# Gate and value products of the second feed-forward layer as seven products of 2x2 blocks

## The chip, the core and the metric

The kernel runs on one core of one Trainium2 chip. The metric is the device time of one execution in microseconds (us); lower is better. The core's engines work side by side and are tied by semaphores: TensorE (PE, its weight loads PEld), VectorE (DVE), ScalarE (ACT), GpSimd (POOL), and SyncE (SP), which issues the DMAs here.

## What is computed

The reference filters two sequences by an FFT and passes the 6016 tokens of 256 channels through two feed-forward layers. The change is in the last one:

```
x = irfft(rfft(x) * F)                      # 2 x 3008 tokens, 256 channels
x = silu(x @ w_in) @ w_out                  # layer 1: 256 -> 2048 -> 256
g, v = x @ w_gate, x @ w_val                # layer 2: 256 -> 1536, twice
out = (silu(g) * v) @ w_out2                # 1536 -> 256
```

## The kernel before

Weights arrive as float64, are rounded to float32 on the chip and split into a high and a low part of type float32r. The activations are split in the same way. A product of two split operands is three matmuls (high by high, high by low, low by high, the list `PARTS`), which add up in PSUM.

Tokens go in 12 blocks of 512 (the last has 384), `NBLK` and `size(t)`. Layer 2 runs block by block; within a block a unit `(2, t, f)` makes 128 of the 1536 hidden features. `m2_in` (L492 to L503) makes a unit's gate in one PSUM bank and its value in another: two halves of the 256 channels by three matmuls is 6 matmuls of 512 columns for each, 12 in all (L427). ACT takes silu of the gate (L499), DVE multiplies by the value (L501), and `split` makes the high part on ACT (L434) and the low part on DVE (L435). `m2_out` multiplies by `w_out2`: for each 128 tokens one matmul of 512 columns (L512) and one of 256 (L516), into four banks that the block keeps until its last unit. Their sums leave by ACT (L525), DVE (L526) and a DMA.

The order is written out in the main loop: unit i's `m2_in`, then the `m2_out` of unit i - 4 (`LAG`). A table `todo` puts other steps ahead of a unit: loading and converting weights (`load_w`, `conv_a`, `conv_b`, `conv_c`), and, for each block of layer 2, `load_x2` and `split_x2` (L488 on ACT, L489 on DVE), ten and five units ahead. Each engine keeps the order in which its instructions were written, so an instruction that waits holds up all that stands behind it on its engine. SP's DMAs form one such order too. Tiles named "mid" come from one pool of 35 buffers; PSUM has four buffers for intermediate results (`psum`) and four for sums (`acc_p`).

All weights of layer 2 are made from float64 while layer 1 runs and stay in SBUF until the end.

Of the kernel before, what the change touches and what calls it, by code (L numbers as in the profile page):

```python
# [92 lines left out]
def fft_filter_mlp_kernel(  # L93
# [39 lines left out]
    csp = cp.tile([P, 2, 352], F32R, name="csp")  # L133
# [16 lines left out]
    # the tensor engine runs at half its clock until it has been busy for a while  # L150
# [8 lines left out]
    t2t = [cp.tile([P, 4, P], F32, name=f"t2t{i}") for i in range(2)]  # L159
# [172 lines left out]
    def s4(c, halves=(0, 1), bank=psum):  # L332
        """Four columns, which one or two blocks of tokens take."""
# [47 lines left out]
    def conv_a(key, q, half, on_act=True):  # L381
# [4 lines left out]
        m = stp.tile([P, 512], U32, tag="m", name="m", bufs=4)  # L386
# [22 lines left out]
    def conv_c(key, q, half):  # L409
# [67 lines left out]
    x2_of = {}  # L477
# [5 lines left out]

    def split_x2(t):
        n = size(t)
        x = mid([P, 2, 512], "xh", F32R), mid([P, 2, 512], "xl", F32R)
        s = x2_of.pop(t)
        nc.scalar.copy(x[0][:, :, :n], s[:, :, :n])  # L488
        nc.vector.tensor_tensor(x[1][:, :, :n], s[:, :, :n], x[0][:, :, :n], op=ALU.subtract)  # L489
        xt_of[t] = x  # L490

    def m2_in(t, f):  # L492
        n = size(t)
        gps = psum("g")
        mm_in(gps, "g", f, xt_of[t], n)
        vps = psum("v")
        mm_in(vps, "v", f, xt_of[t], n)
        u = tp.tile([P, 512], F32, tag="u", name="sg")
        nc.scalar.activation(u[:, :n], gps[:, :n], AF.Silu)  # L499
        u2 = tp.tile([P, 512], F32, tag="u", name="gv")  # L500
        nc.vector.tensor_tensor(u2[:, :n], vps[:, :n], u[:, :n], op=ALU.mult)  # L501
        hid[2, t, f] = split(u2, n)

    def m2_out(t, f):
        nt = size(t) // P
        if f == 0:
# [32 lines left out]
    units += [(2, t, f) for t in range(NBLK) for f in range(12)]  # L539
# [8 lines left out]
    def weights(i, key, q, step=1):  # L548
        """Loads and converts one pair of halves in stages."""
# [23 lines left out]
    for t in range(NBLK):  # L573
        i = begin[2, t]
        at(i - 10, load_x2, t)
        at(i - 5, split_x2, t)
    i = 80
    for key, q in (("g", 0), ("v", 0), ("o2", 0), ("g", 1), ("v", 1), ("o2", 1)):
        weights(i, key, q, 4)
        i += 8  # L580
    for i, key in ((14, "g"), (10, "v"), (6, "o2")):
        weights(END1 - i, key, 2, 2)

    # the second batch's transform, between the units of the first batch's blocks
# [9 lines left out]
    for h in range(12):  # L594
# [15 lines left out]
    LAG = 4  # L610
    with tc.manual_schedule():
# [118 lines left out]
        late["p"] = pool("late", 6)  # L730
# [74 lines left out]
```

## Time and profile before

| what | value |
|---|---|
| timed runs | 1240.48, 1243.15, 1245.9 us; median 1243.15 |
| profiled execution, span from first to last instruction | 1240.2 us |
| PE busy | 1214.2 us, 98% of the span |
| PEld, DVE, ACT, POOL busy | 1008.4, 598.7, 556.8, 170.2 us |
| granted TensorE clock, mean | 0.993 of full speed (2.4 GHz) |
| first gate matmul of layer 2, last DMA issue | 645.3 us, 1236 us after the span's start |

The profile is of one execution, for which a span is given and no device time apart from it; the median of the timed runs lies 2.95 us above that span, for what lies around it. Matmuls are pipelined and their ends are modelled, so the distance from one matmul's start to the next tells what one costs, not its duration.

### The profile page before, as it was taken

Reading aid. Unit: us, or ns where it says so; the run is one execution under the profiler, and the core shown is the slowest. Engines: PE = TensorE matmul, PEld = TensorE weight load, DVE = VectorE, ACT = ScalarE, POOL = GpSimd, SP = SyncE. Lnnn points to the kernel's source line nnn. Section 1 sums busy time; section 2 is a strip of 40 time slices with the busy share of each in tenths; the row PEclk is TensorE's granted clock in tenths of the full one; section 3 lists DMA queues with packets and bytes.
Section 4 is the critical chain, followed back from the end, with each engine's and each line's share of the span. In section 5 each row is a group of like instructions: output and inputs, shape, how many; then the busy total and the mean of one; then the engine's idle time right before and its main releaser. Section 6 shows DMA issues by size and latency. Waiting matters only on the chain.

```text
span 1240.2 us, 14660 instructions
## 1 busy us (share of the span) xinstructions
PE 1214.2 (98%) x5772; PEld 1008.4 (81%) x5772; DVE 598.7 (48%) x890; ACT 556.8 (45%) x985; POOL 170.2 (14%) x120
## 2 busy tenths in 40 slices
PE   7999899999999999999999999999999999999998
PEld 6567678888888888888888888888888888888898
DVE  4889957674354552222384333343343433433433
ACT  3565666665455555444454333233333333333332
POOL 3545633240012210000040000000000000000000
PEclk9999999999999999999999999999999999999999
DMA  9861532332023120010130010000010100000000
GB/s 235 241 194 49 124 110 70 122 89 77 17 69 94 34 77 18 1 43 18 35 119 30 1 34 18 18 35 17 17 35 1 35 17 17 35 17 13 18 1 30
DMA packets 44740, 69.00 MB, mean 56 GB/s; under 512 B 2848, under 2 KB 27936, under 8 KB 44672
## 3 DMA queue, kind: packets, MB, share of 16 engines
q1 hardware_dynamic: 44672, 68.08, 18.5%
q8 instruction: 45, 0.74, 0.3%
q14 instruction: 23, 0.19, 0.0%
HBM read 46.31 MB, written 21.76 MB: 55 GB/s over the span
## 4 chain that ended last, share of the span: by engine, by line
PE 86%; DVE 3%; POOL 3%; issue 2%; ACT 1%; DMA 1%; POOLq 0%; DVEq 0%
PE h L427 17%; PE acc L466 17%; PE g L427 16%; PE v L427 15%; PE acc L512 11%; PE acc L516 5%; PE s L337 2%; PE s L173 2%; POOL m L407 1%; POOL w L417 1%; DMA x<-in_xp_dram 1%; PE s L170 1%; DVE h L435 1%; POOL fl L195 1%; ACT w L416 1%
## 5 line engine op out<-in xcount | busy, mean ns | idle before, releaser
L466 PE MATMUL acc<-h,w 128*128 128x512 f32 (+1 forms) x1152 | 291.2, 388 | 2.7 <-DVE h L435 2.7
L427 PE MATMUL h<-xh,w 128*128 128x512 f32 (+1 forms) x768 | 268.2, 390 | 2.9 <-ACT w L416 1.6
L435 DVE TENSOR_TENSOR h<-u,h 128x512 fp32r<-128x512 f32 (+1 forms) x192 | 149.5, 780 | 219.0 <-ACT h L434 218.6
L466 PEld LDWEIGHTS acc<-h,w 128*128 128x128 f32 x1152 | 216.9, 189 | 45.6 <-DVE h L435 3.1
L501 DVE TENSOR_TENSOR gv<-v,sg 128x512 f32<-128x512 f32 (+1 forms) x144 | 98.0, 680 | 256.2 <-PE v L427 253.8
L512 PE MATMUL acc<-w,h 128*128 128x512 f32 x564 | 204.0, 396 | 0.0
L427 PE MATMUL g<-xh,w 128*128 128x512 f32 (+1 forms) x576 | 200.1, 388 | 2.5 <-ACT u L454 2.5
L427 PE MATMUL v<-xh,w 128*128 128x512 f32 (+1 forms) x576 | 198.1, 384 | 0.0
L434 ACT CAST h<-gv 128x512 fp32r<-128x512 f32 (+1 forms) x144 | 88.1, 612 | 210.0 <-DVE gv L501 210.0
L454 ACT ACTIVATE u<-h 128x512 f32<-128x512 f32 (+1 forms) x192 | 112.5, 586 | 144.7 <-PE h L427 144.5
L427 PEld LDWEIGHTS h<-xh,w 128*128 128x128 f32 x768 | 144.5, 188 | 33.1 <-ACT w L416 2.0
L499 ACT ACTIVATE sg<-g 128x512 f32<-128x512 f32 (+1 forms) x144 | 84.7, 589 | 174.5 <-PE g L427 174.5
L516 PE MATMUL acc<-w,h 128*128 128x256 f32 x564 | 157.9, 280 | 0.0
L427 PE MATMUL h<-xl,w 128*128 128x512 f32 (+1 forms) x384 | 148.4, 386 | 0.0
L435 DVE TENSOR_TENSOR h<-gv,h 128x512 fp32r<-128x512 f32 (+1 forms) x144 | 98.1, 681 | 97.6 <-ACT h L434 97.6
L427 PEld LDWEIGHTS g<-xh,w 128*128 128x128 f32 x576 | 108.0, 188 | 27.3 <-ACT u L454 3.1
L427 PEld LDWEIGHTS v<-xh,w 128*128 128x128 f32 x576 | 107.9, 188 | 21.2
L512 PEld LDWEIGHTS acc<-w,h 128*128 128x128 f32 x564 | 105.9, 188 | 23.7
L434 ACT CAST h<-u 128x512 fp32r<-128x512 f32 (+1 forms) x192 | 117.5, 612 | 6.1
L427 PE MATMUL g<-xl,w 128*128 128x512 f32 (+1 forms) x288 | 112.3, 390 | 0.0
L427 PE MATMUL v<-xl,w 128*128 128x512 f32 (+1 forms) x288 | 110.7, 384 | 0.0
L516 PEld LDWEIGHTS acc<-w,h 128*128 128x128 f32 x564 | 106.4, 189 | 5.0
(69 smaller groups left out, 1002.9 us busy)
## 6 DMA issues: line engine op xcount, KB each, us to landing
raw<-in_w_out_dram SPq DMA_DIRECT2D x14, 512.0 KB, 6.1
zt<-d SPq DMA_DIRECT2D x16, 384.0 KB, 5.0
x<-in_xp_dram SPq DMA_DIRECT2D x15, 384.0 KB, 9.1
d<-z SPq DMA_DIRECT2D x11, 512.0 KB, 3.3
d<-x SPq DMA_DIRECT2D x22, 256.0 KB, 2.1
x<-d SPq DMA_DIRECT2D x11, 512.0 KB, 3.2
out_dram<-ob SPq DMA_DIRECT2D x11, 512.0 KB, 2.9
raw<-in_w_in_dram SPq DMA_DIRECT2D x8, 512.0 KB, 9.6
```

The lines of the kernel that those rows point to most:

```text
L170: nc.tensor.matmul(o, cst[:k, c0:c1], x, start=True, stop=True)
L173: nc.tensor.matmul(o, csp[:k, mp_, c0:c1], x[xp_], start=(i == 0), stop=(i == 2))
L337: nc.tensor.matmul(ps[:, g, 94 * i:94 * (i + 1)], zt_of[c // 4, g][:, 2 * (c % 4) + i, :], c4, start=True, stop=True,)
L427: nc.tensor.matmul(ps[:, :n], wt[key, f // 4, g][:, wpart, o:o + P], x[xpart][:, g, :n], start=(g == 0 and k == 0), stop=(g == 1 and k == 2),)
L434: nc.scalar.copy(h[:, 0, :n], u[:, :n])
L435: nc.vector.tensor_tensor(h[:, 1, :n], u[:, :n], h[:, 0, :n], op=ALU.subtract)
L454: nc.scalar.activation(u[:, :n], ps[:, :n], AF.Silu)
L466: nc.tensor.matmul(acc[1, t][m][:, :n], w[:, wpart, o:o + 128], h[:, xpart, :n], start=(f == 0 and k == 0), stop=(f == 15 and k == 2),)
L499: nc.scalar.activation(u[:, :n], gps[:, :n], AF.Silu)
L501: nc.vector.tensor_tensor(u2[:, :n], vps[:, :n], u[:, :n], op=ALU.mult)
L512: nc.tensor.matmul(a.rearrange("p (l d) -> p l d", l=2), h[:, 0, i * P:(i + 1) * P], w[:, :, f % 2, :], start=(f == 0), stop=False, skip_g ...
L516: nc.tensor.matmul(a[:, D:], h[:, 1, i * P:(i + 1) * P], w[:, 0, f % 2, :], start=False, stop=(f == 11), skip_group_check=True,)
```

## The change

Layer 2's gate and value now use a Strassen form (with the sums shared as in Winograd's variant). Two hidden-feature groups of 128 that lie 256 apart (f and f + 2) and the two halves of a block's tokens form a 2x2 product: weights of 2 channel halves by 2 feature groups, times activations of 2 channel halves by 2 token halves. The plain way takes eight block products, this one seven. A block product is three matmuls of 256 columns instead of being a half of three matmuls of 512.

A unit `m2_unit(t, q, j, outs)` makes both feature groups, so a block has 6 units instead of 12. Per unit PE does 42 matmuls of 256 columns (7 products, 3 parts, gate and value) where two old units had 24 of 512, and the same two `m2_out`. The seven products land in three of the four PSUM buffers (`xs[0]`, `xs[1]`, `y`). What Strassen adds between them is done by ACT (two copies `s` out of PSUM), DVE (`u2`, two additions in place in PSUM, `u3`, the first half of `c`) and POOL (the second half of `c`). The second feature group's silu, product, cast and low part (on POOL) are kept in `rest` and run inside the next unit.

The sums of activations are made by POOL for each block (`prep_x2`, four subtractions of 256 columns, ahead of unit 4 of the block before) and split ahead of unit 5 (`split_x2`, now on 1792 columns instead of 1024). The sums of weights are made during layer 1 on POOL and ACT (`comb_a`, `comb_b`, `comb_c`), written to DRAM (27 DMAs of 512 KB, those of `w_out2` among them), and read back from 18 units before the end of layer 1 on (27 DMAs, `load_2`). The conversions start at the same unit as before (80), and end at unit 173 of the 192 of layer 1. Up to that start all engines' instructions stand as they did. Pools that only the transform and the conversions need are closed earlier to make room.

```diff
     def conv_c(key, q, half):
...
+        if key == "o2":
+            nc.sync.dma_start(do2[q][half], w.rearrange("p l f -> p (l f)").bitcast(F32))
...
+    def comb_a(key, q):
+        v = pair[key, q].bitcast(F32)
+        s = sums[key, q] = mid([P, 4, 256], "ws")
+        sub = lambda o, a, b: nc.gpsimd.tensor_tensor(o, a, b, op=ALU.subtract)
+        nc.gpsimd.tensor_tensor(s[:, 0], v[:, 0, 256:], v[:, 1, 256:], op=ALU.add)
+        sub(s[:, 1], s[:, 0], v[:, 0, :256])
+        sub(s[:, 2], v[:, 0, :256], v[:, 0, 256:])
+        sub(s[:, 3], v[:, 1, :256], s[:, 1])
...
     def split_x2(t):
...
+        for hi, lo, v in (
+            (u[:, 0, :, :n], u[:, 1, :, :n], x[:, :, :n]),
+            (u2[:, 0, :n], u2[:, 1, :n], x[:, 1, n:2 * n]),
+            (h[:, :, :n], l[:, :, :n], r[:, :, :n]),
+        ):
+            nc.scalar.copy(hi, v)
+            nc.vector.tensor_tensor(lo, v, hi, op=ALU.subtract)
...
+    def m2_unit(t, q, j, outs):
...
+        if old:
+            old[0]()
+        for i in range(2):
+            product(xs[i][:, cols[0]], KV[i], q, j, 1, t, first=True)
+            product(xs[i][:, cols[1]], KV[i], q, j, 5, t)
+            nc.scalar.copy(s[:, i, :, :n], xs[i].rearrange("p (l k) -> p l k", l=2)[:, :, :n])
+            if old:
+                old[1 + i]()
...
+        for i in range(2):
+            product(yv[:, i], KV[i], q, j, 6, t, first=(i == 0))
+        nc.vector.tensor_tensor(u2, yv, s[:, :, 0, :n], op=ALU.add)
+        if old:
+            old[3]()
+        outs(0)
+        for i in range(2):
+            product(xs[i][:, cols[0]], KV[i], q, j, 2, t)
+            product(xs[i][:, cols[1]], KV[i], q, j, 3, t, last=True)
+            o = xs[i][:, cols[1]]
+            nc.vector.tensor_tensor(o, o, u2[:, i], op=ALU.add)
...
+        nc.scalar.activation(half(g1), half(xs[0]), AF.Silu)
+        for i in range(2):
+            product(yv[:, i], KV[i], q, j, 7, t)
+        nc.vector.tensor_tensor(u3, yv, s[:, :, 0, :n], op=ALU.add)
+        nc.gpsimd.tensor_tensor(c[:, :, 1, :n], u3, s[:, :, 1, :n], op=ALU.add)
+        nc.vector.tensor_tensor(half(g1), half(xs[1]), half(g1), op=ALU.mult)
+        outs(1)
...
+        nc.scalar.copy(pack(h[:, 0]), half(g1))
+        for i in range(2):
+            product(yv[:, i], KV[i], q, j, 4, t, last=(i == 1))
...
+        def c21():
+            nc.vector.tensor_tensor(c[:, :, 0, :n], yv, s[:, :, 0, :n], op=ALU.add)
+            nc.vector.tensor_tensor(pack(h[:, 1]), half(g1), pack(h[:, 0]), op=ALU.subtract)
...
+        rest.append((c21, silu, cast, low))
...
+    for t in range(1, NBLK):
+        later(t - 1, 3, load_x2, t)
+        later(t - 1, 4, prep_x2, t)
+        later(t - 1, 5, split_x2, t)
```

Line numbers in the rows that follow are those of each kernel's own file. On PE, in the middle of layer 2, one unit of the kernel before is this (L427 the gate `g` and value `v`, L512 and L516 the `m2_out` of an earlier unit):

```order
L427 MATMUL g<-xh,w 128x512
L427 MATMUL g<-xl,w 128x512
L427 MATMUL g<-xh,w 128x512 x2
L427 MATMUL g<-xl,w 128x512
L427 MATMUL g<-xh,w 128x512
L427 MATMUL v<-xh,w 128x512
L427 MATMUL v<-xl,w 128x512
L427 MATMUL v<-xh,w 128x512 x2
L427 MATMUL v<-xl,w 128x512
L427 MATMUL v<-xh,w 128x512
L512 MATMUL acc_6525<-w,h 128x512
```

And the middle of a unit of the changed kernel on PE, from the last matmul of `outs(0)` over the products 2 and 3 to the first of product 7 (`xg`, `xv` are `xs[0]`, `xs[1]`):

```order
L693 MATMUL acc_6755<-w_5632,h 128x256
L602 MATMUL xg<-xu,w_5067 128x256 x3
L602 MATMUL xg<-xu_6987,w_5087 128x256 x2
L602 MATMUL xg<-xu_6987,w_5107 128x256
L602 MATMUL xv<-xu,w_5127 128x256 x3
L602 MATMUL xv<-xu_6987,w_5147 128x256 x2
L602 MATMUL xv<-xu_6987,w_5167 128x256
L602 MATMUL y<-xrh,w_5087 128x256
L602 MATMUL y<-xrl,w_5087 128x256
L602 MATMUL y<-xrh,w_5107 128x256
L602 MATMUL y<-xrh,w_5147 128x256
```

Each product now has its own three matmuls of half the width, and the bank `xg` is written in two visits, with ACT's copy of it between them.

On DVE, at the place where a block's activations are split (L489 before, L589 after), the kernel before has one instruction between two units:

```order
L435 TENSOR_TENSOR h<-gv,h 128x512
L489 TENSOR_TENSOR xl<-x_8274,xh 128x1024
L501 TENSOR_TENSOR gv<-v,sg 128x512
L435 TENSOR_TENSOR h<-gv,h 128x512
```

The changed kernel has three, ahead of the addition L664 (first half of `c`) that the unit before left over:

```order
L650 TENSOR_TENSOR sg<-xv,sg 128x512
L589 TENSOR_TENSOR xu<-x_6807,xu 128x512
L589 TENSOR_TENSOR xu_6987<-x_6807,xu_6987 128x256
L589 TENSOR_TENSOR xrl<-xr,xrh 128x1024
L664 TENSOR_TENSOR c<-y,s 128x2x256
L665 TENSOR_TENSOR h<-sg,h 128x512
L671 TENSOR_TENSOR sg<-c,sg 128x512
L634 TENSOR_TENSOR u_6902<-y,s 128x512
```

On ACT the casts of that split (L588) stand, at the same place, between the last cast of a unit (L658) and the first copy `s` of the next (L627):

```order
L658 CAST h<-sg 128x512
L588 CAST xu<-x_6807 128x512
L588 CAST xu_6987<-x_6807 128x256
L588 CAST xrh<-xr 128x1024
L627 COPY s<-xg 128x512
L668 ACTIVATE sg<-c 128x512
L627 COPY s<-xv 128x512
L672 CAST h<-sg 128x512
```

So a unit's leftover work, and the copies out of PSUM that PE waits for, stand behind the split on both engines.

## Rows read from the trace of the kernel before

**Rows 1.** Windows: stretch, then busy us of PE, PEld, DVE, ACT, POOL (instructions), clock.

```profile
243.00:636.00 393.00, 393.00 (x1843) 331.12 (x1842) 175.13 (x280) 209.17 (x364) 55.09 (x40) 1.00 0.18 55
636.00:690.00 54.00, 51.53 (x253) 44.31 (x252) 28.23 (x40) 23.57 (x42) 7.87 (x6) 1.00 0.08 27
690.00:1192.00 502.00, 502.00 (x2423) 420.72 (x2422) 192.91 (x293) 167.56 (x292) 0.00 (x0) 1.00 0.06 20
800.00:900.00 100.00, 100.00 (x484) 83.80 (x483) 38.31 (x58) 33.31 (x58) 0.00 (x0) 1.00 0.06 22
```

**Rows 2.** Timeline in layer 2, one `m2_out`: start, duration, engine, line.

```profile
901.22 0.39 PE L512 MATMUL acc<-w,h 128*128 128x512 f32 x1
...
901.45 0.28 PE L516 MATMUL acc<-w,h 128*128 128x256 f32 x1
901.45 0.19 PEld L512 LDWEIGHTS acc<-w,h 128*128 128x128 f32 x1
...
901.56 0.40 PE L512 MATMUL acc<-w,h 128*128 128x512 f32 x1
901.57 0.19 PEld L516 LDWEIGHTS acc<-w,h 128*128 128x128 f32 x1
...
902.62 0.40 PE L427 MATMUL g<-xh,w 128*128 128x512 f32 x1
```

**Rows 3.** Timeline of PE in layer 1: eight matmuls of 94 columns, then the next.

```profile
314.64 1.03 PE L337 MATMUL s<-cst,zt 96*128 96x94 f32 x8
315.45 0.48 PE L427 MATMUL h<-xh,w 128*128 128x512 f32 x1
```

**Rows 4.** Timeline of PE in the last block: first of twelve 384-column matmuls, and the thirteenth.

```profile
1192.89 0.34 PE L427 MATMUL g<-xh,w 128*128 128x384 f32 x1
...
1194.97 0.39 PE L512 MATMUL acc<-w,h 128*128 128x512 f32 x1
```

**Rows 5.** Groups by form on ACT: count, busy us, mean ns, idle before.

```profile
L434 ACT CAST h<-gv 128x512 fp32r<-128x512 f32 x132 | 82.0, 621 | 196.2 <-DVE gv L501 196.2
L499 ACT ACTIVATE sg<-g 128x512 f32<-128x512 f32 x132 | 78.8, 597 | 162.5 <-PE g L427 162.5
...
L525 ACT COPY ob<-acc 128x256 f32<-128x256 f32 x47 | 14.1, 381 | 3.3 <-PE acc L516 3.3
...
L488 ACT CAST xh<-x 128x1024 fp32r<-128x1024 f32 x11 | 11.5, 1043 | 0.0
```

**Rows 6.** Groups by form on DVE.

```profile
L435 DVE TENSOR_TENSOR h<-u,h 128x512 fp32r<-128x512 f32 x176 | 140.3, 799 | 211.7 <-ACT h L434 211.3
L435 DVE TENSOR_TENSOR h<-gv,h 128x512 fp32r<-128x512 f32 x132 | 91.4, 692 | 90.6 <-ACT h L434 90.6
...
L526 DVE TENSOR_TENSOR ob<-acc,ob 128x256 f32<-128x256 f32 x47 | 16.6, 415 | 3.1 <-ACT ob L525 3.1
...
L489 DVE TENSOR_TENSOR xl<-x,xh 128x1024 fp32r<-128x1024 f32 x11 | 13.5, 1224 | 2.6 <-ACT xh L488 2.6
```

**Rows 7.** Timeline in layer 2: last gate matmul, and the ACT instruction that waits for it.

```profile
899.63 0.39 PE L427 MATMUL g<-xh,w 128*128 128x512 f32 x1
...
900.12 0.60 ACT L499 ACTIVATE sg<-g 128x512 f32<-128x512 f32 x1 [1.43 <-PE g L427]
```

**Rows 8.** Groups by form on POOL.

```profile
L417 POOL TENSOR_TENSOR w<-m,w 128x512 fp32r<-128x512 f32 x34 | 45.5, 1338 | 37.1 <-ACT w L416 37.1
...
L195 POOL TENSOR_TENSOR fl<-tin,fh 128x1024 fp32r<-128x1024 f32 x6 | 16.6, 2771 | 5.1 <-ACT fh L194 5.1
```

**Rows 9.** Timeline in layer 1: POOL and DVE at the same time, both on SBUF alone.

```profile
257.68 1.28 POOL L290 TENSOR_TENSOR y<-y,t2t 128x512 f32<-128x512 f32 x1 [4.02 <-DVE t2t L286]
258.05 1.47 DVE L435 TENSOR_TENSOR h<-u,h 128x512 fp32r<-128x512 f32 x1 [0.51 <-ACT h L434]
```

**Rows 10.** The page's DMA issues: KB each, us from issue to landing.

```profile
d<-z SPq DMA_DIRECT2D x11, 512.0 KB, 3.3
```

**Rows 11.** Groups by form on PE: a matmul on plain float32.

```profile
L170 PE MATMUL s<-y,cst 128*128 128x512 f32 x24 | 13.6, 649 | 3.6 <-POOL y L290 3.6
```

More of the change, by code (lines that the diff above doesn't have):

```diff
@@ L156, in warm @@
             nc.tensor.matmul(ps[:, :256], idle[:, :P], idle, start=True, stop=True)
-    t2t = [cp.tile([P, 4, P], F32, name=f"t2t{i}") for i in range(2)]
+    t2t = [yp.tile([P, 4, P], F32, name=f"t2t{i}", bufs=1) for i in range(2)]
     PARTS = ((0, 0), (0, 1), (1, 0))
@@ L356, in fft_filter_mlp_kernel @@
     SRC = {"i1": w_in, "o1": w_out, "g": w_gate, "v": w_val, "o2": w_out2}
-    scale_t = [cp.tile([P, 512, 2], U16, name=f"scale{i}") for i in range(3)]
+    scale_t = [stp.tile([P, 512, 2], U16, name=f"scale{i}", bufs=1) for i in range(3)]
     n_half = [0]
-    raws, parts = {}, {}
+    raws, parts, pair = {}, {}, {}
     def load_w(key, q, half):
@@ L385, in conv_a @@
         n_half[0] += 1
-        m = stp.tile([P, 512], U32, tag="m", name="m", bufs=4)
+        if key in ("g", "v"):
+            if half == 0:
+                pair[key, q] = mid([P, 2, 512], "v2", U32)
+            m = pair[key, q][:, half]
+        else:
+            m = stp.tile([P, 512], U32, tag="m", name="m", bufs=4)
         nc.vector.tensor_scalar(m, high, 0xFFFFF, None, op0=ALU.bitwise_and)
@@ new lines, in store, with comb_b @@
+    def store(d, w):
+        nc.sync.dma_start(d, w.bitcast(F32))
+    def comb_b(key, q):
+        v = pair.pop((key, q)).bitcast(F32)
+        w = mid([P, 2, 2, 256], "wa", F32R)
+        nc.scalar.copy(w[:, 0], v[:, :, :256])
+        nc.gpsimd.tensor_tensor(w[:, 1], v[:, :, :256], w[:, 0], op=ALU.subtract)
+        if key == "g":
+            a22[q] = mid([P, 2, 2, 256], "wa2", F32R)
+        k = int(key == "v")
+        nc.scalar.copy(a22[q][:, k, 0], v[:, 1, 256:])
+        nc.gpsimd.tensor_tensor(a22[q][:, k, 1], v[:, 1, 256:], a22[q][:, k, 0], op=ALU.subtract)
+        store(dw[key, q][0], w.rearrange("p l o f -> p (l o f)"))
+        if k:
+            store(dw2[q], a22.pop(q).rearrange("p l o f -> p (l o f)"))
@@ new lines, in comb_c, with load_2 @@
+    def comb_c(key, q):
+        s = sums.pop((key, q))
+        h, l = mid([P, 4, 256], "wsh", F32R), mid([P, 4, 256], "wsl", F32R)
+        nc.scalar.copy(h, s)
+        nc.gpsimd.tensor_tensor(l, s, h, op=ALU.subtract)
+        store(dw[key, q][1], h.rearrange("p o f -> p (o f)"))
+        store(dw[key, q][2], l.rearrange("p o f -> p (o f)"))
+    def load_2(key, q, n):
+        p = late["p"] if q == 2 and key != "o2" and n < 3 else mp
+        w = p.tile([P, 1024], F32R, tag="mid", name="w2")
+        nc.sync.dma_start(w.bitcast(F32), do2[q][n] if key == "o2" else dw2[q] if n == 3 else dw[key, q][n])
+        if key == "o2":
+            wt[key, q, n] = w.rearrange("p (l f) -> p l f", l=2)
+        elif n == 0:
+            wt[key, q, n] = w.rearrange("p (l o f) -> p l o f", l=2, o=2)
+        elif n == 3:
+            wt[q] = w.rearrange("p (k l f) -> p k l f", k=2, l=2)
+        else:
+            wt[key, q, n] = w.rearrange("p (o f) -> p o f", o=4)
@@ L420, in fft_filter_mlp_kernel, with w_op @@
+    def w_op(key, q, j, n, part):
+        c = slice(P * j, P * j + P)
+        if n in (1, 2):
+            return wt[key, q, 0][:, part, n - 1, c]
+        if n == 4:
+            return wt[q][:, int(key == "v"), part, c]
+        return wt[key, q, 1 + part][:, {5: 0, 6: 1, 7: 2, 3: 3}[n], c]
     acc = {}
     hid = {}
+    M2_ORDER = [4 * q + j + k for q in range(3) for j in range(2) for k in (0, 2)]
     def mm_in(ps, key, f, x, n, halves=(0, 1)):
@@ L482, in load_x2, with prep_x2 @@
         nc.sync.dma_start(x2_of[t][:, :, :n], d3[t][:, :, :n])
-    def split_x2(t):
[L485 to L502, printed above, removed]
+    def prep_x2(t):
+        n = size(t) // 2
+        x = x2_of[t]
+        r = mid([P, 4, 256], "xr")
+        b11, b12, b21, b22 = (x[:, k, n * l:n * l + n] for k in range(2) for l in range(2))
+        sub = lambda o, a, b: nc.gpsimd.tensor_tensor(r[:, o, :n], a, b, op=ALU.subtract)
+        sub(0, b12, b11)
+        sub(1, b22, r[:, 0, :n])
+        sub(2, b22, b12)
+        sub(3, b21, r[:, 1, :n])
+        x2_of[t] = x, r
@@ new lines, in product @@
+    def product(o, key, q, j, n, t, first=False, last=False):
+        u, u2, r, m = xop[t]
+        for k, (wpart, xpart) in enumerate(PARTS):
+            if n in (1, 2):
+                x = u[:, xpart, n - 1, :m]
+            elif n == 3:
+                x = u2[:, xpart, :m]
+            else:
+                x = r[xpart][:, {5: 0, 6: 1, 7: 2, 4: 3}[n], :m]
+            nc.tensor.matmul(
+                o, w_op(key, q, j, n, wpart), x, start=(first and k == 0), stop=(last and k == 2),
+                skip_group_check=True,
+            )
@@ new lines, in fft_filter_mlp_kernel, with silu, cast, low @@
+    KV = ("g", "v")
+    rest = []
+    def m2_unit(t, q, j, outs):
+        n = size(t) // 2
+        cols = slice(0, n), slice(256, 256 + n)
+        xs = [psum("xg"), psum("xv")]
+        old = rest.pop() if rest else None
+        s = late2["p"].tile([P, 2, 2, 256], F32, tag="s", name="s", bufs=2)
+        u2, u3 = (
+            late2["p"].tile([P, 2, 256], F32, tag=f"u{i}", name=f"u{i}", bufs=1)[:, :, :n] for i in (2, 3)
+        )
+        c = late2["p"].tile([P, 2, 2, 256], F32, tag="c", name="c", bufs=2)
+        if old:
[6 more added lines that the diff above has]
+                old[1 + i]()
+        y = psum("y")
+        yv = y.rearrange("p (l k) -> p l k", l=2)[:, :, :n]
+        for i in range(2):
[9 more added lines that the diff above has]
+            nc.vector.tensor_tensor(o, o, u2[:, i], op=ALU.add)
+        half = lambda a: a.rearrange("p (l k) -> p l k", l=2)[:, :, :n]
+        g1 = tp.tile([P, 512], F32, tag="u", name="sg")
+        nc.scalar.activation(half(g1), half(xs[0]), AF.Silu)
[5 more added lines that the diff above has]
+        outs(1)
+        hs = [mid([P, 2, 512], "h", F32R) for _ in range(2)]
+        pack = lambda a: a.rearrange("p (l k) -> p l k", l=2) if n == 256 else a[:, :2 * n].rearrange(
+            "p (l k) -> p l k", l=2
+        )
+        h = hs[0]
+        nc.scalar.copy(pack(h[:, 0]), half(g1))
+        for i in range(2):
+            product(yv[:, i], KV[i], q, j, 4, t, last=(i == 1))
+        g2 = tp.tile([P, 512], F32, tag="u", name="sg")
+        def c21():
+            nc.vector.tensor_tensor(c[:, :, 0, :n], yv, s[:, :, 0, :n], op=ALU.add)
+            nc.vector.tensor_tensor(pack(h[:, 1]), half(g1), pack(h[:, 0]), op=ALU.subtract)
+        def silu():
+            nc.scalar.activation(half(g2), c[:, 0, :, :n], AF.Silu)
+        def cast():
+            nc.vector.tensor_tensor(half(g2), c[:, 1, :, :n], half(g2), op=ALU.mult)
+            nc.scalar.copy(pack(hs[1][:, 0]), half(g2))
+        def low():
+            nc.gpsimd.tensor_tensor(pack(hs[1][:, 1]), half(g2), pack(hs[1][:, 0]), op=ALU.subtract)
+        rest.append((c21, silu, cast, low))
+        hid[2, t, 4 * q + j], hid[2, t, 4 * q + j + 2] = hs
@@ L538, in fft_filter_mlp_kernel @@
     END1 = len(units)
-    units += [(2, t, f) for t in range(NBLK) for f in range(12)]
     begin = {}
@@ L572, in fft_filter_mlp_kernel, with weights2, room @@
             at(i - 6 + 2 * k, s4, c)
[L573 to L576, printed above, removed]
-    i = 80
[L578 to L582, printed above, removed]
+    def weights2(i, key, q):
+        weights(i, key, q, 3)
+        if key != "o2":
+            at(i + 6, comb_a, key, q)
+            at(i + 8, comb_b, key, q)
+            at(i + 10, comb_c, key, q)
+    i = 80
+    for q in range(3):
+        for key in ("g", "v", "o2"):
+            weights2(i, key, q)
+            i += 11
+    LAST = i + 6
+    at(LAST, conv_s.close)
+    def room():
+        late2["p"] = pool("late2")
+    at(LAST + 1, room)
+    i = END1 - 18
+    for key, n in (("g", 0), ("g", 1), ("g", 2), ("v", 0), ("v", 1), ("v", 2), ("g", 3)):
+        at(i, load_2, key, 0, n)
+        i += 1
+    at(i, load_2, "o2", 0, 0)
+    at(i, load_2, "o2", 0, 1)
+    at(END1 - 8, load_x2, 0)
+    at(END1 - 5, prep_x2, 0)
+    at(END1 - 3, split_x2, 0)
+    todo2 = {}
+    later = lambda t, k, fn, *args: todo2.setdefault((t, k), []).append((fn, args))
+    for n, (key, m) in enumerate((("g", 0), ("g", 1), ("g", 2), ("g", 3), ("v", 0), ("v", 1), ("v", 2))):
+        at(END1 - 4 + n // 2, load_2, key, 1, m)
+    for q in (1, 2):
+        for n in range(2):
+            later(0, 2 * q - 2, load_2, "o2", q, n)
+    for key, m in (("g", 0), ("g", 1), ("g", 2), ("g", 3), ("v", 0), ("v", 1), ("v", 2)):
+        later(0, 1, load_2, key, 2, m)
+    for t in range(1, NBLK):
+        later(t - 1, 3, load_x2, t)
+        later(t - 1, 4, prep_x2, t)
+        later(t - 1, 5, split_x2, t)
     F0, F1 = Fft(0), Fft(1)
@@ L607, in fft_filter_mlp_kernel @@
             at(i + 4, F1.store_z, q)
+    at(79, fft_s.close)
     WARM = 18
@@ L729, in fft_filter_mlp_kernel @@
         early.close()
-        late["p"] = pool("late", 6)
+        late["p"] = pool("late", 6, side="right")
         for j in range(2):
@@ L753, in fft_filter_mlp_kernel, with outs @@
         at(1, conv_c, "o1", 0, 1)
-        for i in range(len(units) + LAG):
+        for i in range(len(units)):
             for fn, args in todo.pop(i, ()):
                 fn(*args)
-            if i < len(units):
-                l, t, f = units[i]
-                (m1_in if l == 1 else m2_in)(t, f)
+            m1_in(*units[i][1:])
             if i >= LAG:
-                l, t, f = units[i - LAG]
-                (m1_out if l == 1 else m2_out)(t, f)
+                m1_out(*units[i - LAG][1:])
+        pend = [(m1_out, t, f) for _, t, f in units[-LAG:]]
+        def outs(k):
+            for _ in range(max(1, (len(pend) - 1 + k) // 2) if pend else 0):
+                fn, t, f = pend.pop(0)
+                fn(t, f)
+        for i in sorted(todo):
+            for fn, args in todo[i]:
+                fn(*args)
+        for t in range(NBLK):
+            for k in range(6):
+                for fn, args in todo2.pop((t, k), ()):
+                    fn(*args)
+                q, j = divmod(k, 2)
+                m2_unit(t, q, j, outs)
+                pend += [(m2_out, t, 4 * q + j), (m2_out, t, 4 * q + j + 2)]
+        for fn in rest.pop():
+            fn()
+        for fn, t, f in pend:
+            fn(t, f)
 def kernel(x, filt_r, filt_i, moe_w_in, moe_w_out, moe2_w_gate, moe2_w_val, moe2_w_out):
```

35 lines of the change are left out of this document (25 added, 10 removed).

## The prediction

> **What bounds the kernel now.** I read the windows first. In layer 2 PE is busy for 502.0 of 502 us, while DVE has 193, ACT 168 and POOL nothing to do [rows 1]. The same holds in layer 1 from 243 to 636 us: PE 393 of 393, POOL 55 [rows 1]. So from 243 us on only PE's own matmuls set the time, apart from 2.5 us lost around the change of layers (51.53 of 54) [rows 1]. What counts is therefore what one matmul costs from start to start, and whether PE finds its data ready.
>
> A hundred us of layer 2 hold 484 matmuls; a unit has 12 + 8 = 20, so a unit takes 100 / 484 x 20 = 4.13 us, two units 8.26 [rows 1]. An `m2_out`, four pairs of 512 and 256 columns, takes 902.62 - 901.22 = 1.40 [rows 2]. The 12 gate and value matmuls have the other 2.73, which is 0.228 each.
>
> **A product of 256 columns.** The trace has no run of 256-column matmuls one behind the other. The nearest row is the single one in `m2_out`: from 901.45 to 901.56, 0.11 [rows 2]; the mean 256 of a 512 (0.228 / 2) says 0.114. Below, the weight load may bind: the load for the next matmul begins as the 256-column one begins (901.45) and its matmul starts 0.11 later [rows 2], and eight matmuls of 94 columns, each with a load of its own, take 0.81 us, 0.10 each [rows 3]. So a load costs 0.10 to 0.11 at most, just under the 256 columns. I take 0.114, with 0.111 and 0.12 as bounds.
>
> **The product stream.** A new unit has 42 x 0.114 = 4.79 us of products and two `m2_out`, 2.80, together 7.59 against 8.26: 0.67 less. Blocks 0 to 10 have 66 units: **-44.5 us** (-53 at 0.111, -28 at 0.12).
>
> **The last block.** Its tokens come in halves of 192. Twelve matmuls of 384 columns take 2.08 us now, 0.173 each [rows 4]. 192 columns would be worth 0.085, but then the load binds, 0.10 to 0.11. 42 x 0.11 = 4.62 against 24 x 0.173 = 4.16, times 6 units: **+2.8 us** (+0.3 at 0.10).
>
> **Does PE find its data in an ordinary unit?** I count from a unit's first matmul. PE's order: products 1 and 5 until 1.37, product 6 until 2.05, `outs(0)` until 3.45, products 2 and 3 of the gate until 4.13, of the value until 4.82, product 7 until 5.50, `outs(1)` until 6.90, product 4 until 7.58. A result is with the next engine 0.10 after its matmul's modelled end (899.63 + 0.39 to 900.12) [rows 7]; a 256-column matmul lasts 0.28 [rows 2], so that is 0.27 after PE has gone on. Durations: ACT 0.60 to 0.62 for 512 columns, 0.38 for 256, 1.04 for 1024 [rows 5]; DVE 0.69, 0.415 and 1.22 [rows 6].
> DVE: `c` of the unit before 0.27 to 0.96, its low part to 1.65. ACT: copy `s` of the gate 0.95 to 1.55, the silu left over to 2.15, copy of the value to 2.75. DVE: the product left over to 2.85, `u2` to 3.54. PE needs the gate's copy at 3.45, the value's at 4.13, `u2` at 4.82: spare 1.9, 1.4 and 1.3 us. Then `u3`: product 7 is there at 5.77, done 6.46, needed by product 4 at 6.90: spare 0.44, the tightest place. The gate-value product ends at 7.15, the cast behind it at 7.8. Nothing waits, so the unit is 7.59. Per unit ACT has 3.6 us, DVE some 5, POOL 2.7 (two of 1.34) [rows 8]: no engine becomes the bound. The results that leave after a block's last `m2_out` (four copies, four additions) put DVE 1 us behind in one unit, inside those spares.
>
> **Unit 5 of a block.** Here the split for the next block stands in front. ACT: the last cast until 0.2, then 0.62 + 0.38 + 1.04 to 2.24, then the gate's copy to 2.84, in time. DVE: 0.69 and 0.415 to 1.93; the third waits for ACT until 2.24 and takes 1.22, to 3.46; only then `c`, to 4.15. Behind that wait stands ACT's silu (to 4.75), and behind the silu the value's copy, to 5.35. PE wants to write over that bank at 4.13: it waits 1.22. DVE's low part and product end at 5.53, `u2` at 6.22; product 7 is wanted at 6.04: 0.18 more. With the small gaps between engines I take 1.5 us, 11 times (before blocks 1 to 11): **+16.5 us**. The kernel before does 1.04 and 1.22 us at this place [rows 5, 6] and PE loses nothing, because there a bank is written again only two units, 8.26 us, later and no copy stood in between. The lower bound is 0 (the engines run ahead by more than I see), the upper 2 us.
>
> **Layer 1.** The 6 sets of weight sums give POOL four additions of 256 (0.67 each, half of 1.34), 1.34, 0.67 and 2.77 [rows 8], 7.5 us a set, 45 us in all, and ACT some 2 us a set. PE's 393 busy us cover them; POOL had 55, ACT 209 of work there [rows 1]. POOL also delays DVE (below), and the low part of layer 1's hidden features must come within four units of 2.7 us; I give it 0, at most 1 us a set. The 27 stores and 27 loads of 512 KB (a store now lands in 3.3 us [rows 10], and layer 1 uses 18% of the DMA engines, 55 GB/s [rows 1]) go by SP in order. A store waits for POOL and holds up the loads behind it by a few us, but loads of tokens stand four units (11 us) ahead of their use, and the first nine tiles of layer 2 go out 18 to 11 units before it begins. Without that cover nine loads would be 9 x 3.3 = 30 us. What lies at the change of layers stays as it is (2.5 us lost): the conversions leave it, a larger split comes.
>
> **Sum.** -44.5 + 2.8 + 16.5 = -25.2: span 1215.0, and with the 2.95 us that the median lies above the span, 1218 us.
>
> **The rivals.**
> *No stall in unit 5* (0.15). Against it: both splits stand ahead of the leftover work in the order. For it: a split's work could hide if PE is late itself. 1218 - 16.5 = 1201.5.
> *Narrow float32r* (0.06). No float32r matmul under 256 columns is in the trace. A plain float32 one of 512 columns lasts 0.649 against 0.39 [rows 11, 2], 0.26 more; if 192 columns fell to that, 0.085 + 0.10 = 0.185 instead of 0.11, times 252: +19, 1237. That is no change by this kernel's measurement.
> *Products at 0.12 and 1 us lost per weight set in layer 1* (0.09): -28 + 2.8 + 16.5 + 6 = -2.7, 1240.
> *DVE and POOL in each other's way* (0.08), the case on the other side. A DVE instruction on SBUF alone that met a POOL one took 1.47 instead of 0.69 and ended 0.56 after it [rows 9, 6]; layer 2 has POOL work now. If the low part and the leftover product met one in every unit, `u2` would come 1.56 later, at 5.1: PE waits 0.28 in 55 units and the full 1.56 in the 11 with the split, 15.4 + 17.2 = +32.6, 1251. It decides from 0.38 us a unit on (25.2 / 66). Against it: POOL's half of `c` runs 6.46 to 7.8, over before the low part begins at 0.96 of the next unit, and its low part begins when the leftover cast is done, 3.47, when DVE works from PSUM. Only in unit 4, where POOL has the four subtractions, do they meet, inside spares of 1.3 us. The Trainium skill, "SBUF — State Buffer", section "Who interferes with whom", has this as a lock of the shared ports, held for a whole instruction by whichever comes first, and says that a DVE instruction with one input from PSUM is free of it; the pair of rows agrees with the first half.
> *Weight loads add up* (0.04). PEld is 84% busy in layer 2 [rows 1] at 0.19 a load [rows 2]. A new unit has 58 loads, 10.9 us by that count against 7.59: +3.3 x 66 = +218 on the products' path, some 1436. Against it: loads begin 0.12 apart while each lasts 0.19 [rows 2], so they overlap already, and eight took 0.81 [rows 3]. The Trainium skill, "Perfetto Trace Analysis", section "Identifying the Most-Contended Engine", takes that busy share for the measure of TensorE's headroom; by it this change must lose.
>
> **How the numbers follow.** The forecast has 0.58 (1211 to 1227). A change under 0.5%, 6 us, can hardly be told from none. Faster: forecast and no stall, 0.73. Same: narrow float32r and the slow products, 0.15. Slower: 0.12. The range 1203 to 1238 holds the forecast, most of the no-stall case, narrow float32r and half of the slow products, about 0.8.
>
> **What would show it.** Right: 256-column matmuls 0.11 apart in the products; an ordinary unit of 7.6 us with PE never idle; in each sixth unit PE waiting some 1.2 to 1.5 us for ACT's copy of the value (L627); the last block slower than before by some 3 us; layer 1 ending at the same time. Wrong: gaps over 0.12 between products; PE waiting for DVE's `u3` or `u2` in every unit; PE idle in layer 1 after 330 us; DVE instructions of 1.4 us in layer 2.

## The result, and the profile of the changed kernel

The changed kernel takes 1227.47 us (median of four runs, 1225.8 to 1233.66), the kernel before 1243.52 beside it (four runs, 1240.48 to 1245.9): a ratio of 0.9881, with a 95% interval of 0.9854 to 0.9909. The interval lies below 1, so it is faster, by some 1.2%: inside the range of 1203 to 1238, but by less than was forecast. The profiled spans are 1225.2 and 1240.2, 15.0 us apart where the sum said 25.2. In each of the four runs the span lies 1.7 to 1.8 us under the time (1225.2 under 1226.94), so the 2.95 that the forecast added to a span held 1.2 us of spread between runs.

The page of the changed kernel, busy us, share of the span and instructions of each engine:

```profile
PE 1198.5 (98%) x7068; PEld 1049.2 (86%) x7068; DVE 752.6 (61%) x1202; ACT 651.8 (53%) x1171; POOL 443.1 (36%) x354
```

The windows, which answer to [rows 1] (the third ends at 1180, since the whole kernel ends earlier):

```profile
243.00:636.00 393.00, 393.00 (x1817) 327.10 (x1817) 183.60 (x291) 222.12 (x386) 110.39 (x89) 1.00 0.32 106
636.00:690.00 54.00, 54.00 (x383) 52.78 (x382) 30.44 (x51) 27.98 (x51) 17.82 (x16) 1.00 0.47 175
690.00:1180.00 490.00, 484.52 (x3564) 459.31 (x3562) 329.90 (x565) 242.34 (x440) 195.28 (x163) 1.00 0.07 22
800.00:900.00 100.00, 98.90 (x730) 93.84 (x729) 67.03 (x114) 49.64 (x90) 39.25 (x34) 1.00 0.07 22
```

POOL's work in layer 1 has doubled (110.39 against 55.09 in [rows 1]), and PE is still busy for 393 of 393 us. The 2.5 us that PE lost around the change of layers are gone (54.00 of 54). In layer 2 PE is idle for 5.5 us of 490. The view of PE's waits in that third window (us in all, times, longest) has one row:

```profile
PE xv L602 <- ACT s L627: 5.5, 10, 0.6
```

That is the wait forecast for unit 5: PE, which wants the value's bank again, waits for ACT's copy of it. It comes ten times, once in each of blocks 0 to 9, and PE waits for nothing else there. The timeline of PE over the first 18 matmuls of an ordinary unit (start, duration, line; the unit ahead began at 807.6):

```profile
815.46 0.52 PE L602 MATMUL xg<-xu,w 128*128 128x256 f32 x3
815.82 0.28 PE L602 MATMUL xg<-xrh,w 128*128 128x256 f32 x1
...
816.18 0.52 PE L602 MATMUL xv<-xu,w 128*128 128x256 f32 x3
...
817.62 0.40 PE L689 MATMUL acc<-w,h 128*128 128x512 f32 x1
```

Eighteen products of 256 columns take 817.62 - 815.46 = 2.16 us: 0.120 each, not 0.114. With 42 of them and two `m2_out` of 1.40 the unit is 7.84 us, not 7.59. The last block starts at 1174.58, and its 18 products of 192 columns take 1.99 us, 0.110 each, as foretold:

```profile
1174.58 0.48 PE L602 MATMUL xg<-xu,w 128*128 128x192 f32 x3
...
1176.57 0.42 PE L689 MATMUL acc<-w,h 128*128 128x512 f32 x1
```

Unit 5 of a block on all engines (`m2_out` and weight loads are left out; a bracket holds the idle time ahead and what ended it):

```profile
831.01 0.92 ACT L588 CAST xu<-x 128x512 fp32r<-128x512 f32 x2
831.07 0.52 PE L602 MATMUL xg<-xu,w 128*128 128x256 f32 x3
...
831.84 1.05 ACT L588 CAST xrh<-xr 128x1024 fp32r<-128x1024 f32 x1
...
832.80 0.57 ACT L627 COPY s<-xg 128x512 f32<-128x512 f32 x1
832.93 1.23 DVE L589 TENSOR_TENSOR xrl<-xr,xrh 128x1024 fp32r<-128x1024 f32 x1 [0.24 <-ACT xrh L588]
...
834.07 0.69 DVE L664 TENSOR_TENSOR c<-y,s 128x512 f32<-128x512 f32 x1
834.61 0.87 PE L602 MATMUL xg<-xu,w 128*128 128x256 f32 x6
...
834.87 0.63 ACT L668 ACTIVATE sg<-c 128x512 f32<-128x512 f32 x1 [1.50 <-DVE c L664]
835.41 0.57 ACT L627 COPY s<-xv 128x512 f32<-128x512 f32 x1
836.03 0.97 PE L602 MATMUL xv<-xu,w 128*128 128x256 f32 x6 [0.56 <-ACT s L627]
836.15 0.68 DVE L634 TENSOR_TENSOR u<-y,s 128x512 f32<-128x512 f32 x1
836.88 0.39 PE L602 MATMUL y<-xrh,w 128*128 128x256 f32 x1
...
837.11 0.28 PE L602 MATMUL y<-xrl,w 128*128 128x256 f32 x1
...
839.83 0.40 PE L602 MATMUL xg<-xu,w 128*128 128x256 f32 x2
```

The chain is the one that the prediction walked: third cast, third low part, `c`, silu, the value's copy, PE. The unit takes 839.83 - 831.07 = 8.76 us, 0.92 over an ordinary one. In block 10, where the split for the narrower last block stands, it takes 1174.58 - 1166.50 = 8.08, 0.24 over. Ten of the one and one of the other make 9.4 us, not 16.5.

Where the 15.0 us come from, by spans:

| part | forecast | measured |
|---|---|---|
| start to layer 2's first product | 0 | 645.31 to 649.74: +4.4 |
| unit 5, eleven times | +16.5 | +9.4 |
| product stream, blocks 0 to 10 | -44.5 | -31.0 |
| wait at the change of layers, the part behind that first product | 0 | -1.2 |
| last block and end | +2.8 | 47.3 to 50.6: +3.3 |
| sum | -25.2 | -15.1 |

Blocks 0 to 10 took 1192.89 - 645.31 = 547.6 before, 1.2 of it waiting, and take 1174.58 - 649.74 = 524.8 now, 9.4 of it in the stalls: 546.4 and 515.4 without either, hence -31.0. The parts add up to 0.1 more than the two spans' distance, by rounding.

### The profile page after: what moved, and what is told of

Read it like the earlier page. It is cut to its first block, busy times and chain, and to the rows that moved or that the text cites. A ratio compares the mean times of both kernels' runs of the same rounds, so it can differ in the third digit from the quotient of the medians.

```text
span 1225.2 us, 18420 instructions
## 1 busy us (share of the span) xinstructions
PE 1198.5 (98%) x7068; PEld 1049.2 (86%) x7068; DVE 752.6 (61%) x1202; ACT 651.8 (53%) x1171; POOL 443.1 (36%) x354
## 4 chain that ended last, share of the span: by engine, by line
PE 82%; DVE 5%; ACT 3%; issue 2%; POOL 2%; DMA 1%; POOLq 0%; DVEq 0%; ACTq 0%
PE h L507 19%; PE acc L546 19%; PE y L602 11%; PE acc L689 9%; PE xv L602 8%; PE xg L602 7%; PE acc L693 5%; PE s L346 2%; PE s L182 2%; DVE xrl L589 1%; PE s L179 1%; ACT xrh L588 1%; DMA x<-in_xp_dram 1%; ACT xu L588 1%; POOL m L421 1%
## 5 line engine op out<-in xcount | busy, mean ns | idle before, releaser
L602 PE MATMUL y<-xrh,w 128*128 128x256 f32 (+1 forms) x864 | 190.0, 283 | 0.0
L675 POOL TENSOR_TENSOR h<-sg,h 128x512 fp32r<-128x512 f32 (+1 forms) x72 | 91.4, 1270 | 227.9 <-ACT h L672 226.6
L602 PEld LDWEIGHTS y<-xrh,w 128*128 128x128 f32 x864 | 148.2, 189 | 4.0
L649 POOL TENSOR_TENSOR c<-u,s 128x512 f32<-128x512 f32 (+1 forms) x72 | 91.6, 1272 | 130.2 <-DVE u L648 128.0
L602 PE MATMUL y<-xrl,w 128*128 128x256 f32 (+1 forms) x432 | 121.5, 281 | 0.0
L602 PE MATMUL xv<-xu,w 128*128 128x256 f32 (+1 forms) x648 | 101.5, 283 | 5.5 <-ACT s L627 5.5
L602 PE MATMUL xg<-xu,w 128*128 128x256 f32 (+1 forms) x648 | 100.1, 281 | 0.0
L602 PEld LDWEIGHTS xv<-xu,w 128*128 128x128 f32 x648 | 87.2, 190 | 7.6 <-ACT s L627 7.5
L658 ACT CAST h<-sg 128x512 fp32r<-128x512 f32 (+1 forms) x72 | 44.1, 613 | 92.0 <-DVE sg L650 92.0
L645 ACT ACTIVATE sg<-xg 128x512 f32<-128x512 f32 (+1 forms) x72 | 42.5, 590 | 94.5 <-DVE xg L642 94.5
```

The source lines that it names most:

```text
L602: nc.tensor.matmul(o, w_op(key, q, j, n, wpart), x, start=(first and k == 0), stop=(last and k == 2), skip_group_check=True,)
L645: nc.scalar.activation(half(g1), half(xs[0]), AF.Silu)
L649: nc.gpsimd.tensor_tensor(c[:, :, 1, :n], u3, s[:, :, 1, :n], op=ALU.add)
L658: nc.scalar.copy(pack(h[:, 0]), half(g1))
L675: nc.gpsimd.tensor_tensor(pack(hs[1][:, 1]), half(g2), pack(hs[1][:, 0]), op=ALU.subtract)
```

## The experiments

The open points: what a 256-column product costs and why; where layer 1 lost 4.4 us; whether unit 5's stall is all that the split costs; and whether the spare of 0.44 at product 7 is as tight as was counted. Each paragraph names the kernel to which its edit is made.

**e1_halves: the kernel before, with each gate and value matmul of 512 columns as two of 256.** The work in columns is the same, so only a cost per matmul can show. The rival was that a 256 costs half of a 512 and that the changed kernel's 0.120 comes from its own order.

```diff
+        cuts = ((0, n // 2), (n // 2, n)) if key in ("g", "v") else ((0, n),)
...
+                for a, e in cuts:
+                    nc.tensor.matmul(
+                        ps[:, a:e], wt[key, f // 4, g][:, wpart, o:o + P], x[xpart][:, g, a:e],
```

> The kernel before, with each gate and value matmul of 512 columns cut into two of 256 that load the same weights; nothing else changes, and no Strassen work is there. Theory A (a matmul costs its columns at 2.4 GHz plus a fixed 0.013 us, so one of 256 costs 0.120 wherever it stands): a unit of layer 2 goes from 4.13 to 24 x 0.120 + 1.40 = 4.28 us, the last block by the weight loads from 3.12 to 24 x 0.110 + 1.04 = 3.68; over 132 and 12 units that is 20 + 7, a span of some 1267 us. Theory B (256 columns cost 0.114, and the 0.12 of the changed kernel comes from ACT, DVE and POOL working beside the products): units stay at 4.13 and only the last block grows, a span of some 1247 us.

Measured: 1264.49 us in one execution, against 1244.0 for the kernel before beside it; span 1262.7, some 4 under Theory A, of which 3.1 is a layer 2 that began earlier here (642.2 us for 645.3). The timeline of PE at the start of a gate, and the windows:

```profile
903.59 0.40 PE L429 MATMUL g<-xh,w 128*128 128x256 f32 x2
903.83 0.40 PE L429 MATMUL g<-xl,w 128*128 128x256 f32 x2
...
905.03 0.40 PE L429 MATMUL v<-xh,w 128*128 128x256 f32 x2
```

```profile
800.00:900.00 100.00, 100.00 (x748) 95.76 (x747) 37.65 (x58) 32.73 (x57) 0.00 (x0) 1.00 0.07 22
```

Twelve matmuls in 905.03 - 903.59 = 1.44 us, 0.120 each, with PE never idle. So 0.120 is what a 256-column matmul with a weight load of its own costs, in either kernel; the rival is out, since nothing of Strassen's runs beside the matmuls here. Two of them cost 0.012 more than one of 512 (0.228).

**e2_late_aligned and e3_before_shifted: where layer 1's time went.** Layer 1's matmuls are the same in both kernels, and PE is busy throughout, yet layer 1 took longer. Among what differs is the address of the pool `late`, six of the eight tiles of `w_in`, which takes the place of the pool `zp`: 201408 bytes into a partition before, 204768 in the changed kernel, which is 32 bytes past a multiple of 64. Two kernels turn this round. In e2 the changed kernel gets a pad of 32 bytes ahead of that pool:

```diff
     early = ExitStack()
+    padp = pool("padp", side="right")
+    pad = padp.tile([P, 8], F32, name="pad")
     zp = early.enter_context(tc.tile_pool(name="zp", bufs=1, side="right"))
```

> The changed kernel with 32 bytes per partition left free above the pool of late weights, so that its tiles begin at multiples of 64 bytes instead of 32 past one; no instruction changes. Theory A (weights that begin 32 bytes past a multiple of 64 make a 512-column matmul 3 to 8 ns longer, and three quarters of layer 1's first matmuls have such weights): the first matmul of layer 2 starts at 645 to 646 us instead of 649.7, and the span is some 4.5 us shorter, 1220 to 1222. Theory B (the weight sums, stores and loads added to layer 1 slow it, or the two profiles differ by chance): the start stays near 649 to 650 and the span near 1225.

In e3 the kernel before gets the same pad, so that its weights come to lie 32 bytes off:

```diff
     early = ExitStack()
+    pad = pool("padp").tile([P, 8], F32, name="pad")
     zp = early.enter_context(tc.tile_pool(name="zp", bufs=1))
```

> The kernel before with 32 bytes per partition put ahead of the pool of late weights, so that its tiles begin 32 bytes past a multiple of 64; no instruction changes. Theory A (the weights' address): layer 1 gets some 4.5 us longer, its six late weight tiles show 230 to 235 ns from start to start instead of 227, and layer 2, which has weights there too, may add to it; a span of 1243 to 1247. Theory B (not the address): no change, span 1240.

Measured: e2 1223.05 us (1222.62 to 1227.85), ratio to the kernel before 0.9835 (0.9819 to 0.9852); e3 1247.37 us (1245.23 to 1248.94), ratio 1.0032 (1.0019 to 1.0045). The profiled execution of e2 was the longest of its four; it started its layer-1 matmuls some 5 us later than the changed kernel did, so its first product of layer 2 came at 649.9 and not at the 645 to 646 that Theory A expected, and its span of 1226.0 isn't the one to compare. What compares is a stretch inside layer 1: first to last start of the 94-column matmuls of one line, between 250 and 640 us, by a view of that line (changed kernel, e2, e3):

```profile
L346 PE MATMUL s<-cst,zt x168: 245/275/275, 265.4 to 603.5; 96*128 96x94 f32 x168
```

```profile
L348 PE MATMUL s<-cst,zt x168: 245/275/275, 269.4 to 604.1; 96*128 96x94 f32 x168
```

```profile
L338 PE MATMUL s<-cst,zt x168: 245/275/275, 263.0 to 601.1; 96*128 96x94 f32 x168
```

338.1 us in the changed kernel, 334.7 with the pad; the kernel before took 334.6 (263.4 to 598.0) and takes 338.1 with its weights shifted. These 3.4 us go with the 32 bytes alone, in both kernels, and the weight sums on POOL and ACT with their stores cost PE nothing in this stretch. (Their loads come from 609 us on, where PE doesn't wait either.)

That it is the weights' address, and nothing else that the pad moves, the changed kernel shows by itself. Two units of one block in layer 1, the first matmul of each and the one behind its six: the first unit's weights are the last that don't lie in `late`, the second's the first that do.

```profile
576.97 0.39 PE L507 MATMUL h<-xh,w 128*128 128x512 f32 x1
...
578.33 1.53 PE L546 MATMUL acc<-h,w 128*128 128x512 f32 x6
579.70 0.39 PE L507 MATMUL h<-xh,w 128*128 128x512 f32 x1
...
581.09 1.53 PE L546 MATMUL acc<-h,w 128*128 128x512 f32 x6
```

Six matmuls take 1.36 us, then 1.39: 0.227 and 0.232 each. In the kernel before and in e2 both kinds of unit take 1.36, and in e3 they take 1.36 and 1.39 again. Products of 256 columns don't show it: in layer 2 of the changed kernel six tiles of weights lie in `late` too, and a product with these takes 0.119, one with others 0.120. Why an address costs TensorE time no run shows.

**e4_split_spread: the changed kernel, with the split of the next block cut into four pieces.** They stand behind the gate-value product of units 3, 4 (two) and 5, where ACT and DVE have room, in place of all ahead of unit 5. The rival was that what the split costs would only come up somewhere else.

```diff
-    def m2_unit(t, q, j, outs):
+    def m2_unit(t, q, j, outs, between=()):
...
+        for fn, args in between:
+            fn(*args)
         outs(1)
...
-        later(t - 1, 5, split_x2, t)
+        for k, which in ((3, (0,)), (4, (1, 2)), (5, (3,))):
+            inside.setdefault((t - 1, k), []).append((split_x2, (t, which)))
```

> The changed kernel with the split of the next block's activations cut into four pieces, which stand in units 3, 4 and 5 behind the unit's gate-value product instead of all ahead of unit 5's leftover work. Theory A (PE's wait in each sixth unit comes from that place in the order of ACT and DVE, and DVE has 0.9 us free behind the product): unit 5 falls from 8.75 to 7.85 us, PE waits nowhere in layer 2, the span is 9 to 10 us shorter, 1215 to 1216. Theory B (DVE's work in a block is what PE waits for, wherever it stands): the wait is spread over units 3 to 5 or moves to product 4's wait for u3, and the span stays within 3 us of 1225.

Measured: 1217.57 us (1216.82 to 1220.1), ratio 0.9796 (0.9781 to 0.981), span 1215.4, 9.8 less than the changed kernel's. Its windows:

```profile
690.00:1180.00 490.00, 490.00 (x3643) 467.58 (x3642) 353.71 (x588) 248.21 (x461) 202.19 (x166) 1.00 0.07 22
```

PE waits for nothing in layer 2 any more, with the same split on the same engines. So the 9.4 us of the table come from where the split stood and from the size of its pieces, which e4 changes together, and not from the amount of work in it.

**e5_spread_aligned: both, e2's pad and e4's pieces.** The edit is the sum of those two.

> Both edits together: late weights at multiples of 64 bytes and the split spread over units 3 to 5. Theory A (two separate costs, 3.7 us of layer 1 and some 10 us of layer 2): the sum of both, a median some 13 us under the changed kernel's 1227, 1213 to 1215; layer 1 takes as long as in the kernel before and PE waits nowhere in layer 2. Theory B (one hides behind the other, or the address gains nothing in the whole): 1217 to 1218, as with the spread split alone.

Measured: 1215.08 us (1213.11 to 1215.51), ratio 0.9766 (0.9752 to 0.9779), span 1213.4. It lies 12.4 us under the changed kernel, where some 13 were expected. So the two gains add up in the main, though the pad's part beside e4 is 2.5 us (1217.57 to 1215.08) and not 3.4. This version beats the kernel before and the changed one (ratio 0.9881, upper end of its interval here below the lower end there).

**e6_u3_twice: e5 with `u3` computed twice.** It puts another DVE instruction into the tightest place, product 7 to `u3` to product 4, whose spare the prediction counted as 0.44.

```diff
         nc.vector.tensor_tensor(u3, yv, s[:, :, 0, :n], op=ALU.add)
+        nc.vector.tensor_tensor(u3, yv, s[:, :, 0, :n], op=ALU.add)
```

> The same kernel with the addition u3 on DVE written twice in each unit, so that product 4 gets its bank some 0.6 us later. Theory A (the chain product 7, u3, product 4 has 0.4 to 0.5 us to spare, as counted): PE waits 0.1 to 0.2 us for DVE at product 4 in each ordinary unit, 7 to 14 us in all. Theory B (there is more to spare than counted): no wait, no change of the span, some 1211 to 1213.

Measured: 1240.08 us in one execution, span 1238.3, 24.9 over e5's: more than either figure that was expected. The timeline of one unit:

```profile
813.08 0.69 DVE L660 TENSOR_TENSOR u<-y,s 128x512 f32<-128x512 f32 x1 [0.29 <-PE y L614]
...
813.81 0.69 DVE L661 TENSOR_TENSOR u<-y,s 128x512 f32<-128x512 f32 x1
...
814.16 0.28 PE L708 MATMUL acc<-w,h 128*128 128x256 f32 x1
814.42 0.68 DVE L663 TENSOR_TENSOR sg<-xv,sg 128x512 f32<-128x512 f32 x1
814.56 0.39 PE L614 MATMUL y<-xrh,w 128*128 128x256 f32 x1
...
814.78 0.28 PE L614 MATMUL y<-xrl,w 128*128 128x256 f32 x1
```

The second addition starts 0.73 after the first, once that has ended, and ends at 814.50. Product 4 could have begun at 814.28 (0.12 behind the last `m2_out` matmul) and begins at 814.56: 0.28 late. The matmul behind it comes 0.22 later instead of 0.12: another 0.10. That makes 0.38 a unit, and 66 x 0.38 = 25. So the place is as tight as counted (0.73 added, 0.45 of it free), but the expectation missed that a second addition costs its full time and that PE loses 0.1 when it starts again.

## Why the prediction was right in kind and 10 us off

**A product of 256 columns: the step that failed.** It took 0.114, the half of a 512, as its value and 0.12 as its upper bound; the bound was the truth (e1: 0.120 in the kernel before too). The rows held it: a 512 costs 0.228 [rows 1, 2], a 384 0.173 [rows 4], so 128 columns are worth 0.055, and a line through the two gives 0.173 - 0.055 = 0.118 for a 256. The step halved a cost of which about 0.012 doesn't shrink with the columns. The single 256 in `m2_out`, 0.11 [rows 2], was one start read to a hundredth, too coarse to tell the two apart. The Trainium skill, "TensorE: Matmul & The Clock Gate", section "Back-to-back issue gap", gives for an isolated matmul the columns over 2.4 GHz and 2.5 ns, 109 ns for 256, and says itself that a stream of weight loads and matmuls goes by another spacing; the stream here has 120, and the measurement decides.

**The product stream.** Mis-sized by that step: -31.0 us, near the -28 that the prediction gave for 0.12. (A unit took 8.28 us on average and takes 7.81, 546.4 and 515.4 over 66, where -28 goes by 8.26 and 7.84.) That seven products replace eight and that this is what the kernel gains holds.

**Does PE find its data in an ordinary unit?** Right: the view of waits has no row for one, and e6 measured the spare at product 4 as 0.45 where 0.44 was counted.

**Unit 5 of a block.** The wait, its place and its chain were right, and the rival without a stall is out. The size was 9.4 us, not 16.5, for three reasons that the rows above show. The casts begin 0.06 ahead of the unit's first matmul (831.01 and 831.07), where 0.2 behind it was counted. Instructions that follow one another without waiting start before the one ahead has ended: the two casts take 0.92 together, where 0.62 + 0.38 were added, the value's copy starts 0.54 after the silu's start, and `c` starts 1.14 after an instruction that lasts 1.23. So ACT's copy begins 835.41 - 831.07 = 4.34 after the unit's start, not 4.75. And PE, slower by the first step, wants the bank at 4.26, not 4.13. It resumes at 836.03, where 835.33 was its turn: 0.70. The rest of the 0.92 is 0.1 for this restart (its six matmuls last 0.97, the six ahead of the wait 0.87), some 0.03 for `u2` (836.88, where 836.85 was PE's turn) instead of 0.18, and 0.1 for the second restart (836.88 to 837.11). That the total came within 10 us owes something to luck: this term was 7.1 us too long while the product stream was 13.5 too short. The Trainium skill, "ScalarE: Activation LUTs", section "What ACT_TABLE_LOAD costs", has back-to-back activations overlap by about 93 ns; here ACT's overlap is 0.08 to 0.09.

**The last block.** +3.3 for +2.8. 0.110 for 192 columns is the load's price that was assumed; whether it is the load that binds there was not tested by itself.

**Layer 1.** What the step feared did not come: the sums and stores are hidden, as e2 shows, and PE stays busy through the loads (54.00 of 54). What came instead it had not thought of: 3.4 us by the address of the weights (e2, e3). Another 2.0 lie ahead of the first of those matmuls (263.4 and 265.4), and -1.3 is the first half of the 2.5 us at the change of layers, which the step left in place and which are gone; no run tests why. With 0.3 unaccounted that makes +4.4. The 2.0 can't be told from the start of an execution, which differs from one to the next: the same line begins between 260.2 and 269.4 in the profiles of the eight kernels.

**The rivals.** *Narrow float32r*: out, 192 columns cost 0.110 and not 0.185. *Slow products and a loss in layer 1*: half right, with products at 0.12, but its 6 us of weight sets were 3.4 us of address, and the stall that it kept was smaller. *DVE and POOL in each other's way*: out as a cost, though they do meet, in the one unit that the prediction named; see the rows below. *Weight loads add up*: out; loads are busy for 95.76 of 100 us in e1 and PE is not idle. By the share of weight loads, one of two measures of headroom in the Trainium skill, "Perfetto Trace Analysis", section "Identifying the Most-Contended Engine", e4 and the kernel before differ as 95% and 84%, and e4 is the faster.

The meeting of DVE and POOL, in unit 4 of a block of the changed kernel:

```profile
825.35 0.74 POOL L570 TENSOR_TENSOR xr<-x 128x256 f32<-128x256 f32 x1
825.42 1.22 DVE L671 TENSOR_TENSOR sg<-c,sg 128x512 f32<-128x512 f32 x1 [0.63 <-ACT sg L668]
826.05 1.19 POOL L570 TENSOR_TENSOR xr<-x,xr 128x256 f32<-128x256 f32 x1
```

Beside POOL's subtractions the leftover product on DVE takes 1.22 us; the same instruction takes 0.69 in unit 5 (835.54). It is as long in unit 4 of each of blocks 0 to 9, and PE waits for nothing there: the spare of 1.3 us that was counted holds.

## What to carry to other kernels

When a change cuts matmuls into narrower ones, take the price of a width from a line through two widths in the trace, not from a proportion: halving a 512 left out half of a fixed 0.012 us on each of 2,772 matmuls, some 17 us by that count, and 13.5 of the forecast gain of 44.5 did not come. Ahead of a wait on the critical engine, ask of the work queued there whether any of it could stand elsewhere; cut in pieces and spread over three units, the same split cost nothing (e4). After a change of the pools' layout compare the starts of unchanged matmuls, since an address alone moved 3.4 us here.

## What the runs showed of the hardware that was not expected

- Weights that start 32 bytes past a multiple of 64 cost TensorE time in matmuls of 512 columns, 0.232 against 0.227 us: 338.1 against 334.7 us over the same stretch of layer 1, in two kernels and both directions. In products of 256 columns they cost none (0.119 and 0.120).
- A float32r matmul with a weight load of its own costs about 0.012 us beside its columns (0.228 for 512, 0.120 for 256), and 0.110 at 192 columns, more than that line gives.
- After a wait PE's first matmul is followed 0.22 to 0.23 us later, not 0.12, by the next: 0.1 for each wait, beside the wait itself (e6; 836.88 and 837.11 in unit 5).
- The second of two DVE additions on the same tiles started 0.73 after the first, while the unlike instruction behind it started 0.61 after it (813.08, 813.81 and 814.42 in e6).
